# A delta-rule and gated-MLP kernel: filler stages beside lone tile stages, a higher fill level, and a smaller weight for the widening products in the planner

## The chip, the cores and the metric

The kernel runs on one core of one Trainium2 chip. The metric is the device time of one execution in microseconds. TensorE (PE) does the matmuls, VectorE (DVE), ScalarE (ACT) and GpSimd (POOL) the rest, and SyncE (SP) issues the DMAs.

## The reference

Four batches of eight heads, 768 positions, head size 48, and behind them a gated MLP with mixing over the positions:

```
k_n = k / (norm(k) + 1e-6)
for t in range(768):                         # per batch and head, state is 48x48
    y[t]  = q[t] @ state
    state = state + beta[t] * outer(k_n[t], v[t] - k_n[t] @ state)
x = y, heads side by side                    # (4, 768, 384)
h = relu(x @ w_in);  u, v = halves of h      # 1024 -> 512 and 512
v_n = (v - mean(v)) / sqrt(var(v) + 1e-6)
v_s = w_spatial @ v_n + b_spatial            # mixes the 768 positions
out = (u * v_s) @ w_out
```

## The kernel before

**Chunks and steps.** The positions are cut into 12 chunks of 64 for each batch, so there are 48 steps (a step is one chunk of one batch, with its eight heads), and a table sets their order. Four steps are a group. For each group the keys are normed (`norm`), `kk` multiplies the keys with themselves, and the triangular 64x64 matrices of the chunk are inverted: DVE solves 32x32 blocks row by row (`lanes`, lines 647 and 654, with its data taken through DRAM by DMA: `ad`, `la`, `w`, `wd`, `ta`), for the first group in 16x16 blocks (`lanes16`, lines 1158 and 1165), which `widen` puts together with small 32x16 and 16x16 products on TensorE (lines 1192 and 1203). A step then runs the stages e and f (they finish the inverse), a (keys by the state), b (the inverse by the values, tiles `kv,ta`), c (the new state), qk and d (the output). In each batch a stage a waits for the c of the chunk before it.

**Tile stages.** Each of these stages is a list of 8 matmuls (16 for d) of 64x64 tiles in float32, which all write one of four PSUM banks (`pt`, taken and given back through `Slots` by the name `st_s`), and DVE or ACT reads the bank. Each float32 matmul shows as two matmul records in the trace. The two heads of a pair lie on one diagonal of the 128x128 array or on the other, so a stage is of the kind "diag" or "anti". When one stage of each kind is ready, the planner issues the two lists interleaved, one matmul of this, one of that.

**The MLP** works in full 128x128 products: v (line 923), u (line 989), g (lines 1021 and 1024) and o (line 1076), as soon as their positions are through the steps, into the banks `pm` and later `pw`.

**The order** of all instructions comes from a planner in the kernel (`Line`), which holds a model of each engine's time and always issues what can begin first, so each engine's queue is fixed when the kernel is built. Its model of TensorE's clock is a sum over the last 3.4 us (`area`): a full product counts 2300 for each modelled microsecond, a tile matmul 1.3 times its columns, a filler 256. Above `HOT` (3050) it takes matmuls to last 1x, else 2x. Where it sees TensorE wait by more than 0.12 us, and `area` is under `FILL`, it puts in fillers (`keep_warm`, `idle`): 128x256 matmuls of ones into a free bank, which nobody reads.

Of the kernel before, what the change touches and what calls it, by code (L numbers as in the profile page):

```python
# [14 lines left out]
NB, NH, SEQ, HD = 4, 8, 768, 48  # L15
# [25 lines left out]
PAIR = 1.0  # L41
LOW = 3600
HOT = 3050
FILL = 4000


def step_order():
# [19 lines left out]
class Op:  # L67
# [4 lines left out]
    def __init__(self, eng, occ, lat, dep, due, kind=None, make=None):  # L72
        self.eng, self.occ, self.lat, self.dep, self.due = eng, occ, lat, dep, due
        self.kind, self.make = kind, make


class Line:
# [4 lines left out]
    def __init__(self, t0):  # L82
        self.t = dict.fromkeys(("PE", "DVE", "ACT", "POOL", "SP"), t0)
        self.done = {}
        self.jobs = []
        self.mode = "full"
        self.cur = 0
        self.hist = []
        self.idle = self.room = None

    def at(self, *names):
        done = self.done

        def when():
            t = 0.0
            for n in names:
                if n is None:
                    continue
                if n not in done:
                    return None  # L100
                t = max(t, done[n])
            return t

        return when
# [39 lines left out]
    def keep_warm(self, t):  # L144

        n = 0
        while t - self.t["PE"] > 0.12 and self.area(self.t["PE"]) < FILL:
            slow = self.slow(self.t["PE"])
# [8 lines left out]
    def tensor(self, e0, near):  # L157
        tiles = [f for f in near if f[1].kind != "full"]
        full = [f for f in near if f[1].kind == "full"]

        def first(fs):
            return min(fs, key=lambda f: (f[1].due(), f[0]), default=None)

        kinds = {k: [f for f in tiles if f[1].kind == k] for k in ("anti", "diag")}
        low = self.area(e0) < LOW
        room = self.room(2)
        old = [f for f in tiles if e0 - f[3] > HOLD and f[1].due() <= self.cur + URGENT]
        pick = first(full) if low else None
        if pick is None and all(kinds.values()) and room is not None and room <= e0 + 0.3:
            if self.mode == "tile" or not full or old or first(tiles)[1].due() <= self.cur + PAIR:  # L170
                pick = first(tiles)
        pick = pick or first(old) or first(full) or first(tiles)
        t, op, j, _ = pick
        self.keep_warm(t)
        t = max(t, self.t["PE"])
        change = 0.12 if (op.kind == "full") != (self.mode == "full") else 0.0
        slow = self.slow(t)
        if op.kind == "full":
            self.mode = "full"
            self.t["PE"] = t + change + op.occ * slow  # L180
            self.hist.append((self.t["PE"], op.occ * 2300))
            return self.grant(j, t + change + op.occ * slow + op.lat - op.occ)
        self.mode = "tile"
        other = kinds["anti" if op.kind == "diag" else "diag"]
        f = None
        if room is not None and room <= t + 0.2:
            f = first([f for f in other if f[0] <= t + 0.2])
        picked = [(op, j)]
        if f:
            picked.append(f[1:3])  # L190
            t = max(t, f[0], room)
        lists = [o.make() for o, _ in picked]
        act_ = sum(o.lat * len(x) for (o, _), x in zip(picked, lists))
        for k in range(max(map(len, lists))):
            for x in lists:
                if k < len(x):
                    x[k]()
        end = t + change + 0.056 * slow * max(map(len, lists))
        self.t["PE"] = end
        self.hist.append((end, act_))  # L200
        for _, k in picked:
            self.grant(k, end + 0.22)
# [6 lines left out]
def dve(dep, due, e, fast=1.0):  # L209
    return Op("DVE", 0.078 + 0.00104 * e * fast, 0.2 + 0.00104 * e * fast, dep, due)  # L210


def act(dep, due, e, each=0):
    o = 0.05 + 0.15 * each + 0.00098 * e
    return Op("ACT", o, 0.12 + o, dep, due)
# [23 lines left out]
def delta_rule_gated_mlp(  # L239
# [16 lines left out]
    def sb(name, *shape, dt=F32):  # L256
        return const.tile([128, *shape], dt, name=name)

    line = Line(T0)
# [3 lines left out]
    mpos = sb("mpos", CH)  # L263
# [87 lines left out]
    pws = [ps.tile([128, 512], F32, name=f"pw{i}") for i in range(2)]  # L351

    class Slots:
        def __init__(self, tiles):
            self.free = [(0.0, k, x) for k, x in enumerate(tiles)]

        def ready(self, n=1):
            return sorted(self.free)[n - 1][0] if len(self.free) >= n else None

        def take(self):  # L360
            f = min(self.free)
            self.free.remove(f)
            return f[1:]

        def give(self, x, t):
            self.free.append((t, *x))

    st_s = Slots([x[:, 0:256] for x in banks])
    line.room = st_s.ready
    ob_s = Slots([sb(f"ob{i}", DM) for i in range(1)])  # L370
    tmp_s, pm_s, xs_s, vh_s, ub_s = Slots(tmps), Slots(pms), Slots(xsb), Slots(list(zip(vhs, vls))), Slots(ubs)

    def both(*whens):
        def when():
            t = 0.0
            for w in whens:
                x = w()
                if x is None:
                    return None
                t = max(t, x)  # L380
            return t

        return when

    def on(t):
        return lambda: t

    def due(x):
        return lambda: x
# [7 lines left out]
    def rows_t(h):  # L397
        return slice(h * 64, h * 64 + 64)

    def rows_s(h):  # L400
        return rows_t(1 - h)

    UH = [(u, h) for u in range(NU) for h in range(2)]
# [7 lines left out]
    def psl(t, w):  # L411
        return t[:, : NU * w].rearrange("p (u e) -> p u e", e=w)

    def mm(*a, **k):
        return lambda: nc.tensor.matmul(*a, **dict(dict(start=True, stop=True), **k))  # L415

    def tiles_op(kind, dep, d, build, w):

        held = []

        def make():
            x = st_s.take()
            held.append(x)
            return build(psl(x[1], w))

        return Op("PE", 0, 1.3 * w, both(dep, st_s.ready), d, kind, make), held


    def load_w(buf, hi, lo, src, d):
# [74 lines left out]
    def ta_of(g):  # L504
        return tas[g % TG]
# [398 lines left out]
    xuse, vt, ut_t, g_t, todo, own = {}, {}, {}, {}, [], []  # L904
# [275 lines left out]
    def widen(s, buf, pi):  # L1180
        d = due(-5 + s)
        ta = ta_of(0)
        tr = buf[:, s % 2 * 256 : s % 2 * 256 + 256].rearrange("p (u t) -> p u t", t=CH)
        t = yield dve(at(("back", min(s, 1)), ("wp", s - 2) if s > 1 else None), d, 256)
        nc.vector.transpose(out=tr.rearrange("p u t -> p (u t)"), in_=ta[:, s].rearrange("p u t -> p (u t)"))
        t = yield Op("PE", 0.7, 1.0, both(on(t), pm_s.ready), d, "full")
        p = pm_s.take()
        pp, px = (p[1][:, o : o + 64].rearrange("p (u t) -> p u t", t=16) for o in (0, 64))
        for u in range(NU):
            for q in range(4):  # L1190
                r, c = q * 32, q % 2 * 32
                nc.tensor.matmul(
                    pp[r : r + 32, u], ta[r : r + 16, s, u, c : c + 32], tr[r : r + 16, u, c : c + 16],
                    start=True, stop=True,
                )
        done["wp", s] = t
        t = yield act(on(t), d, 64, 1)
        nc.scalar.mul(out=pi[:, s], in_=pp, mul=hm)
        t = yield Op("PE", 0.45, 0.75, on(t), d, "full")
        for u in range(NU):  # L1200
            for q in range(4):
                r, c = q * 32, q % 2 * 32
                nc.tensor.matmul(
                    px[r : r + 16, u], pi[r : r + 32, s, u], ta[r : r + 32, s, u, c + 16 : c + 32],
                    start=True, stop=True,
                )
        for q in range(4):
            r, c = q * 32, q % 2 * 32
            t = yield act(on(t), d, 64)
            nc.scalar.copy(out=ta[r : r + 16, s, :, c + 16 : c + 32], in_=px[r : r + 16])  # L1210
        pm_s.give(p, t)
        done["T", 0, s] = t
# [41 lines left out]


    def idle(t):
        free = [f[2][:, 0:256] for k in (pm_s, st_s) for f in k.free if f[0] <= t]
        if free:
            nc.tensor.matmul(
                free[0].rearrange("p (n t) -> p n t", t=128),  # L1260
                ones,
                ones.unsqueeze(1).broadcast_to([128, 2, 128]),
                start=True,
                stop=True,
            )
        return bool(free)

    line.idle = idle
    ET = mybir.EngineType
    with tc.manual_schedule(engines={ET.PE, ET.DVE, ET.Activation, ET.Pool, ET.SP}):  # L1270
        seen = {"s": 0, "g": 0}
# [75 lines left out]
```

## Time and profile before

| what | value |
|---|---|
| median of 3 runs | 564.54 us (561.43 to 565.8) |
| profiled execution | 563.41 us |
| its span, first to last instruction | 561.7 us |
| mean granted TensorE clock in the span | 0.917 |
| matmul records / weight loads | 9040 / 9040 |
| TensorE, VectorE, ScalarE, GpSimd busy | 500.4, 355.0, 218.9, 142.7 us |

The span is what the trace covers; 1.7 us of the execution lie around it. Matmuls are pipelined, and a busy TensorE may run at half or at full granted clock, which the row PEclk shows apart from the busy share.

### The profile page before, as it was taken

To read this page: it belongs to the slowest core of one execution; us is meant where nothing else is said; L and a number is where in the kernel's file an instruction comes from. 1 tells how busy PE (TensorE), PEld (TensorE's weight loads), DVE (VectorE), ACT (ScalarE), POOL (GpSimd) and SP (SyncE) were. 2 spreads that over 40 slices of the span, in tenths; PEclk is the share of its full clock that TensorE was granted. 3 is DMA by queue.
4 is the path that set the end of the run, shared out by engine and by line. 5 is a ranking of instruction groups with operands and counts; after the bars stand their busy time and mean duration, and the time that the engine had idled before them with its cause. 6 is when DMAs were issued, how large, how long until landed. Compare 5 with 4: busy or idle time off the path is not lost.

```text
span 561.7 us, 21394 instructions
## 1 busy us (share of the span) xinstructions
PE 500.4 (89%) x9040; PEld 451.8 (80%) x9040; DVE 355.0 (63%) x1434; ACT 218.9 (39%) x536; POOL 142.7 (25%) x212
## 2 busy tenths in 40 slices
PE   4936886987989989888989999999999999999997
PEld 4835775876777978788978789879987999898996
DVE  5899786976799978778958993258235341134210
ACT  3233433542636335423235645321256341137111
POOL 5534333653454341323213233311001000000000
PEclk8576695985989989989999999999999999999999
DMA  8687286768575738676865544461304010000001
GB/s 236 175 154 169 92 216 126 215 191 167 139 196 133 191 98 182 147 211 139 207 109 115 136 109 117 134 160 48 67 30 127 17 36 29 32 20 15 2 34 52
DMA packets 134252, 66.97 MB, mean 119 GB/s; under 512 B 105894, under 2 KB 123532, under 8 KB 134156
## 3 DMA queue, kind: packets, MB, share of 16 engines
q1 hardware_dynamic: 134156, 65.60, 47.9%
q8 instruction: 71, 1.16, 0.9%
q14 instruction: 25, 0.20, 0.1%
HBM read 50.11 MB, written 15.17 MB: 116 GB/s over the span
## 4 chain that ended last, share of the span: by engine, by line
PE 60%; DVE 16%; DMA 10%; ACT 4%; issue 4%; SPq 4%; POOL 1%; DVEq 0%; ACTq 0%
PE pt L415 20%; PE pm L1021 11%; PE pm L923 6%; PE pm L989 6%; PE pw L1021 5%; PE pm L1076 4%; PE pw L1076 3%; DVE pw L654 2%; DVE prod L647 2%; DMA knn<-in_k_nat 2%; PE pw L923 1%; DMA k<-in_kv_t 1%; DMA la<-ad 1%; SPq L631 1%; PE pw L989 1%
## 5 line engine op out<-in xcount | busy, mean ns | idle before, releaser
L654 DVE TENSOR_TENSOR pw<-pw,prod 128x96 f32<-128x96 f32 (+7 forms) x330 | 80.7, 250 | 4.6
L647 DVE TENSOR_TENSOR prod<-pw,la 128x126 f32<-128x126 f32 (+7 forms) x330 | 78.3, 242 | 7.9 <-ACT pw L641 2.9
L696 POOL TENSOR_TENSOR kv<-kv,cn 128x192 f32<-128x192 f32 x48 | 24.6, 513 | 142.8 <-DMA kv<-in_kv_t 122.8
L1021 PE MATMUL pm<-wsp_h,vh 128*128 128x256 f32 x204 | 60.2, 295 | 0.4 <-ACT vh L965 0.4
L415 PE MATMUL pt<-kv,st 48*64 48x64 f32 x768 | 55.5, 238 | 4.1 <-ACT ta L737 2.0
L1021 PE MATMUL pm<-wsp_h,vl 128*128 128x256 f32 x204 | 57.7, 283 | 0.2 <-DVE vl L969 0.2
L1021 PE MATMUL pm<-wsp_l,vh 128*128 128x256 f32 x204 | 57.7, 283 | 0.0
L415 PE MATMUL pt<-aq,us 64*64 64x64 f32 x768 | 53.4, 232 | 0.3 <-issue 0.3
L415 PEld LDWEIGHTS pt<-kv,st 48*64 48x64 f32 x768 | 44.0, 147 | 6.9 <-ACT ta L737 2.1
L415 PE MATMUL pt<-kv,ta 64*64 64x48 f32 x768 | 35.5, 231 | 10.4 <-DVE t L550 3.5
L415 PEld LDWEIGHTS pt<-aq,us 64*64 64x64 f32 x768 | 44.3, 148 | 0.4 <-issue 0.4
L415 PEld LDWEIGHTS pt<-kv,ta 64*64 64x64 f32 x768 | 29.7, 143 | 16.3 <-issue 5.8
L1038 DVE TENSOR_TENSOR tmp<-pm,ub 128x512 f32<-128x512 f32 x17 | 11.8, 691 | 48.8 <-PE pm L1024 48.8
L1057 ACT CAST gh<-tmp 128x512 fp32r<-128x512 f32 x24 | 14.8, 618 | 71.0 <-DVE tmp L1038 71.0
L415 PE MATMUL pt<-kv 48*64 48x64 f32 x768 | 35.7, 235 | 6.3 <-DVE t L546 4.7
L415 PE MATMUL pt<-k 48*64 48x64 f32 x640 | 29.4, 232 | 13.1 <-DVE nr L556 8.8
L1021 PEld LDWEIGHTS pm<-wsp_h,vh 128*128 128x128 f32 x204 | 38.8, 190 | 1.9 <-ACT vh L965 0.6
L415 PE MATMUL pt<-tn,ta 64*64 64x32 f32 x768 | 35.3, 234 | 5.2 <-DVE tn L711 3.8
L572 POOL TENSOR_TENSOR mc<-mpos,cn 128x256 f32<-128x256 f32 x46 | 28.6, 628 | 42.9 <-DVE ta L607 24.3
L1021 PEld LDWEIGHTS pm<-wsp_h,vl 128*128 128x128 f32 x204 | 39.0, 191 | 0.4 <-DVE vl L969 0.4
L1021 PEld LDWEIGHTS pm<-wsp_l,vh 128*128 128x128 f32 x204 | 39.0, 191 | 0.0
L415 PEld LDWEIGHTS pt<-tn,ta 64*64 64x64 f32 x768 | 30.7, 149 | 8.9 <-ACT wstage L442 3.8
(176 smaller groups left out, 1426.8 us busy)
## 6 DMA issues: line engine op xcount, KB each, us to landing
kv<-in_kv_t SPq DMA_DIRECT2D x48, 456.0 KB, 4.5
ad<-ta SPq DMA_DIRECT2D x24, 256.0 KB, 4.2
la<-ad SPq DMA_DIRECT2D x44, 128.0 KB, 4.4
out<-ob SPq DMA_DIRECT2D x24, 192.0 KB, 1.9
k<-in_kv_t SPq DMA_DIRECT2D x20, 224.0 KB, 3.9
knn<-in_k_nat SPq DMA_DIRECT2D x10, 384.0 KB, 5.6
wd<-w SPq DMA_DIRECT2D x22, 128.0 KB, 3.9
ta<-wd SPq DMA_DIRECT2D x44, 64.0 KB, 3.5
```

The costliest lines, as they stand in the source:

```text
L415: return lambda: nc.tensor.matmul(*a, **dict(dict(start=True, stop=True), **k))
L572: (nc.vector if t in (0, 2) else nc.gpsimd).tensor_tensor(out=mc, in0=mall, in1=cns[t // G][:, t % G, 1].unsqueeze(2).broadcast_to([128, N ...
L631: nc.sync.dma_start(out=las[g % 2][l0 : l0 + 32], in_=src[:, r0 : r0 + 32, r0 : r0 + 32])
L647: nc.vector.tensor_tensor(out=pr, in0=w[:, :n, j : j + 1].broadcast_to([128, n, m]), in1=la[:, j, j + 1 : 32].unsqueeze(1).broadcast_to([1 ...
L654: nc.vector.tensor_add(out=w[:, :n, j + 1 : 32], in0=w[:, :n, j + 1 : 32], in1=pr)
L696: nc.gpsimd.tensor_tensor(out=v, in0=v, in1=cns[s // G][:, s % G, 0].unsqueeze(2).broadcast_to([128, NU, HD]), op=ALU.mult)
L923: nc.tensor.matmul(p[1], a[:, kt, ts], w[:, kt, DH:], start=(n == 0), stop=(n == 3 * NK - 1))
L989: nc.tensor.matmul(pu[:, k], w[:, kt, d0 : d0 + 128], a[:, kt], start=(n == 0), stop=(n == 3 * NK - 1))
L1021: nc.tensor.matmul(pg[:, k], v[:, d0 : d0 + 128], w[:, si, ts], start=(n == 0), stop=False)
L1038: nc.vector.tensor_tensor(out=gt, in0=pg, in1=ut[:, hs], op=ALU.mult)
L1057: nc.scalar.copy(out=gh[:, hs], in_=gt)
L1076: nc.tensor.matmul(p[1][:, :DM], a[:, dd, ts], w[:, dd], start=(n == 0), stop=(n == 3 * ND - 1))
```

## The change

Four edits, all in the planner and in what it issues:

- `FILL` goes from 4000 to 5000.
- A tile stage that is issued without a partner, while `area` is under the new `FAKE` (5500), gets a filler stage (`fake`): as many matmuls of the mask `mpos` by itself, on the other diagonal, interleaved, into a free bank that nobody reads. That bank keeps a tag, and until it is taken again only stages of the same kind may take it; the general fillers leave it out.
- A stage therefore asks for a bank that fits its kind (`ready_for`), and a pair for two that fit (`ready_both`).
- The two products of `widen` count 150 instead of 2300 for each modelled microsecond in `area`.

```
-FILL = 4000
+FILL = 5000
+FAKE = 5500
...
-        room = self.room(2)
+        room = self.room()
...
-            self.hist.append((self.t["PE"], op.occ * 2300))
+            self.hist.append((self.t["PE"], op.occ * (op.make or 2300)))
...
+        if not f and self.area(t) < FAKE:
+            more = self.fake("anti" if op.kind == "diag" else "diag", t, len(lists[0]))
+            if more:
+                lists.append(more)
+                act_ += 62 * len(more)
...
+        def fit(self, kind):
+            return sorted(f for f in self.free if self.tag.get(f[1], kind) == kind)
...
+        def ready_both(self):
+            a, d = self.fit("anti"), self.fit("diag")
+            t = [max(x[0], y[0]) for x in a for y in d if x[1] != y[1]]
+            return min(t) if t else None
...
-        def take(self):
-            f = min(self.free)
+        def take(self, kind=None):
+            f = min(self.free) if kind is None else self.fit(kind)[0]
             self.free.remove(f)
+            self.tag.pop(f[1], None)
             return f[1:]
...
-        t = yield Op("PE", 0.7, 1.0, both(on(t), pm_s.ready), d, "full")
+        t = yield Op("PE", 0.7, 1.0, both(on(t), pm_s.ready), d, "full", 150)
...
-        t = yield Op("PE", 0.45, 0.75, on(t), d, "full")
+        t = yield Op("PE", 0.45, 0.75, on(t), d, "full", 150)
...
+    def fake(kind, t, n):
+        fit = [f for f in st_s.fit(kind) if f[0] <= t]
+        own = [f for f in fit if f[1] in st_s.tag]
+        if not own and (kind in st_s.tag.values() or len(st_s.free) < 2):
+            return None
+        f = (own or fit or [None])[-1]
+        if f is None:
+            return None
+        st_s.tag[f[1]] = kind
+        p = psl(f[2], HD)
+        r = [
+            mm(p[rows_t(h) if kind == "diag" else rows_s(h), u], mpos[rows_t(h)], mpos[rows_t(h), 0:HD])
+            for u, h in UH
+        ]
+        return (r * 2)[:n]
```

In the whole program the fillers of ones go from 152 to 253, and 29 filler stages (232 matmuls of `mpos`) come in; every other matmul is there as often as before. Since the planner's model changes, all queues after the first microseconds are in another order. Three places on TensorE's queue follow; lines of the changed kernel are 23 higher there (438 is 415 of before, 1215 and 1226 are 1192 and 1203, 1282 is 1259).

Near the start, behind the two products qk of the first steps (`kv_167`, `kv_168`), where the keys of the second group (`xs`) are multiplied. Before:

```order
L415 MATMUL pt_203<-kv_167 64x64 x8
L415 MATMUL pt_204<-kv_168 64x64 x8
L1259 MATMUL pm_207<-ones 128x256 x11
L415 MATMUL pt_205<-xs 64x64 x8
L415 MATMUL pt_203<-xs 64x64 x8
L1259 MATMUL pm_207<-ones 128x256 x6
L415 MATMUL pt_206<-xs 64x64 x8
L1259 MATMUL pm_207<-ones 128x256
L415 MATMUL pt_204<-xs 64x64 x8
```

And now:

```order
L438 MATMUL pt_204<-kv_168 64x64 x8
L1282 MATMUL pm_207<-ones 128x256 x17
L438 MATMUL pt_205<-xs 64x64
L438 MATMUL pt_204<-mpos 64x48
L438 MATMUL pt_205<-xs 64x64
```

The fillers ahead of the next kk went from 11 to 17, and that kk has a filler stage beside it, whose rows alternate with its own.

Ahead of and within `widen` of the first group (lines 1192 and 1203 before), which ends the preparation of the first step. Before:

```order
L1259 MATMUL pm_207<-ones 128x256 x16
L415 MATMUL pt_205<-k 64x64 x8
L1192 MATMUL pm_207<-ub_150,ta_177 32x16 x16
L1192 MATMUL pm_208<-ub_150,ta_177 32x16 x16
L1203 MATMUL pm_207<-ta_177,ub_150 16x16 x16
L1203 MATMUL pm_208<-ta_177,ub_150 16x16 x16
L415 MATMUL pt_203<-k 64x64 x8
L1192 MATMUL pm_207<-ub_150,ta_177 32x16 x16
L1192 MATMUL pm_208<-ub_150,ta_177 32x16 x16
L415 MATMUL pt_206<-tn_175,ta_177 64x32 x8
L1203 MATMUL pm_207<-ta_177,ub_150 16x16 x16
L415 MATMUL pt_204<-tn_176,ta_177 64x32 x8
```

And now:

```order
L1282 MATMUL pm_207<-ones 128x256 x20
L1215 MATMUL pm_207<-ub_150,ta_177 32x16 x16
L1282 MATMUL pm_208<-ones 128x256 x6
L1226 MATMUL pm_207<-ta_177,ub_150 16x16 x16
L1215 MATMUL pm_208<-ub_150,ta_177 32x16 x16
L1282 MATMUL pt_206<-ones 128x256 x2
L1215 MATMUL pm_207<-ub_150,ta_177 32x16 x16
L1226 MATMUL pm_208<-ta_177,ub_150 16x16 x16
L1226 MATMUL pm_207<-ta_177,ub_150 16x16 x16
L438 MATMUL pt_204<-tn_175,ta_177 64x32
L438 MATMUL pt_206<-k 64x64
L438 MATMUL pt_204<-tn_175,ta_177 64x32
```

A run of 20 fillers now stands directly ahead of it, where a kk did (with 16 fillers ahead of that kk), 8 fillers stand within it, and its products come one step at a time instead of two steps together.

Behind stage b (`kv_168,ta_180`) of the step that is 13th counted from 0, the second of the second batch. Before:

```order
L1259 MATMUL pm_207<-ones 128x256 x5
L415 MATMUL pt_204<-kv_168,ta_180 64x48 x8
L415 MATMUL pt_206<-k 64x64 x8
L415 MATMUL pt_205<-tn_176,ta_180 64x32 x8
L415 MATMUL pt_204<-us_116,kv_168 64x48 x8
L1259 MATMUL pm_207<-ones 128x256
L415 MATMUL pt_205<-kv_168,st_112 64x64 x2
```

And now:

```order
L438 MATMUL pt_206<-kv_168 64x64 x8
L438 MATMUL pt_204<-kv_168,ta_180 64x48 x8
L1282 MATMUL pm_207<-ones 128x256 x10
L438 MATMUL pt_203<-kv_169 64x64 x8
L438 MATMUL pt_205<-us_116,kv_168 64x48 x8
L1282 MATMUL pm_207<-ones 128x256 x3
L438 MATMUL pt_204<-k 64x64 x8
L1282 MATMUL pm_207<-ones 128x256 x17
L946 MATMUL pm_207<-win_h,xh 128x512 x3
```

Thirty fillers stand between that b and the next product of the MLP (line 946, 923 before), where one stood behind b and five ahead of it.

More of the change, by code (lines that the diff above doesn't have):

```diff
@@ L88, in __init__ @@
         self.hist = []
-        self.idle = self.room = None
+        self.idle = self.room = self.fake = None
     def at(self, *names):
@@ L355, in __init__, with ready_for @@
             self.free = [(0.0, k, x) for k, x in enumerate(tiles)]
+            self.tag = {}
+        def fit(self, kind):
+            return sorted(f for f in self.free if self.tag.get(f[1], kind) == kind)
         def ready(self, n=1):
             return sorted(self.free)[n - 1][0] if len(self.free) >= n else None
-        def take(self):
-            f = min(self.free)
+        def ready_for(self, kind):
+            f = self.fit(kind)
+            return f[0][0] if f else None
+        def ready_both(self):
[4 more added lines that the diff above has]
+            f = min(self.free) if kind is None else self.fit(kind)[0]
             self.free.remove(f)
+            self.tag.pop(f[1], None)
             return f[1:]
@@ L368, in delta_rule_gated_mlp @@
     st_s = Slots([x[:, 0:256] for x in banks])
-    line.room = st_s.ready
+    line.room = st_s.ready_both
     ob_s = Slots([sb(f"ob{i}", DM) for i in range(1)])
@@ L421, in make @@
         def make():
-            x = st_s.take()
+            x = st_s.take(kind)
             held.append(x)
             return build(psl(x[1], w))
-        return Op("PE", 0, 1.3 * w, both(dep, st_s.ready), d, kind, make), held
+        return Op("PE", 0, 1.3 * w, both(dep, lambda: st_s.ready_for(kind)), d, kind, make), held
     def load_w(buf, hi, lo, src, d):
@@ L1256, in idle @@
     def idle(t):
-        free = [f[2][:, 0:256] for k in (pm_s, st_s) for f in k.free if f[0] <= t]
+        free = [f[2][:, 0:256] for k in (pm_s, st_s) for f in k.free if f[0] <= t and f[1] not in k.tag]
         if free:
@@ L1266, in idle @@
         return bool(free)
-    line.idle = idle
+    def fake(kind, t, n):
[13 more added lines that the diff above has]
+        return (r * 2)[:n]
+    line.idle, line.fake = idle, fake
     ET = mybir.EngineType
```

## Prediction

> **What bounds the kernel now.** I read the page first (size, busy shares, granted clock, chain), then the windows by stage, then the stretches at half clock, and at last what the chain holds in them.
>
> ```profile
> span 561.7 us, 21394 instructions
> PE 500.4 (89%) x9040; PEld 451.8 (80%) x9040; DVE 355.0 (63%) x1434; ACT 218.9 (39%) x536; POOL 142.7 (25%) x212
> PEclk8576695985989989989999999999999999999999
> PE 60%; DVE 16%; DMA 10%; ACT 4%; issue 4%; SPq 4%; POOL 1%; DVEq 0%; ACTq 0%
> ```
>
> TensorE is the engine to look at: 89% busy and 60% of the chain that ended last. But its clock digit is under 9 in most of the first 12 slices and almost always 9 later. So the kernel has two regimes, and the windows (span, then busy of PE, PEld, DVE, ACT, POOL, then granted clock) show where they meet:
>
> ```profile
> 0.00:61.50 61.50, 38.56 (x656) 35.28 (x658) 49.85 (x184) 19.59 (x54) 25.48 (x66) 0.67 0.74 176
> 61.50:151.60 90.10, 74.69 (x1700) 65.05 (x1699) 68.48 (x305) 41.20 (x106) 39.51 (x46) 0.79 0.70 168
> 151.60:354.80 203.20, 187.88 (x4021) 166.60 (x4021) 163.13 (x722) 89.69 (x222) 68.26 (x86) 0.97 0.62 146
> 354.80:482.40 127.60, 124.54 (x2113) 113.03 (x2112) 53.86 (x178) 45.10 (x106) 9.49 (x14) 1.00 0.26 71
> 482.40:561.70 79.30, 74.77 (x560) 71.82 (x560) 19.65 (x47) 23.32 (x50) 0.00 (x0) 0.99 0.08 27
> ```
>
> The stretches end at stage b of step 0, 12, 35 and 47. Up to 61.5 us VectorE is the fuller engine (49.85 of 61.50 us). From 354.8 us on TensorE is 96% busy at a clock of 0.99 to 1.00, and both orders hold the same work there: behind step 35 the same products within one or two stages, behind step 47 the same o, g, v and u, with 12 more fillers of ones and one filler stage. **So those last 207 us move as a block.** What the change can win or lose is when step 35 is reached, and most of that lies before 250 us, where the clock is at half (the third column from the end is the granted clock):
>
> ```profile
> 48.17:65.24 17.07, 12.26 (x423) 11.18 (x425) 13.21 (x55) 9.00 (x31) 3.84 (x6) 0.50 0.51 118
> 68.65:72.07 3.42, 3.29 (x94) 3.33 (x96) 2.17 (x13) 0.84 (x3) 2.28 (x4) 0.50 0.26 71
> 85.72:99.37 13.65, 10.02 (x150) 9.00 (x151) 9.47 (x48) 5.38 (x13) 5.57 (x7) 0.50 0.67 130
> 123.27:140.33 17.06, 13.07 (x275) 11.79 (x271) 10.36 (x35) 5.59 (x17) 4.70 (x8) 0.50 0.84 195
> 164.23:171.05 6.82, 5.94 (x71) 4.54 (x70) 6.58 (x23) 2.01 (x6) 4.52 (x5) 0.50 0.84 168
> 198.36:201.77 3.41, 3.41 (x91) 3.11 (x87) 2.25 (x12) 0.89 (x4) 2.18 (x3) 0.50 0.00 0
> 246.15:249.56 3.41, 3.41 (x121) 3.41 (x112) 2.31 (x8) 1.65 (x6) 0.51 (x1) 0.50 0.55 159
> ```
>
> Busy time at half clock is not all on the path. The chain's shares, asked for the stretch 10.63 to 27.69 us (also half clock) and for these seven in turn, say how much is:
>
> ```profile
> by line: PE pt L415 24.4%; PE pm L1259 15.5%; DVE ta L607 11.7%; DVE mc L572 7.1%; issue 6.8%; DVE ss L539 5.8%; DVE ub L454 4.8%; DVE wstage L458 4.8%; POOL wstage L462 4.3%; DVE ub L460 2.2%; DVE wstage L460 2.0%; DVE wstage L454 2.0%; DV
> by line: PE pt L415 46.0%; issue 21.8%; PE pm L1192 14.8%; PE pm L1203 7.5%; ACT ub L1198 3.8%; PE pm L1259 3.0%; DVE ub L1185 2.6%; DVE prod L647 1.7%; DVE pw L654 0.2%
> by line: PE pt L415 98.4%; DVE prod L647 3.5%; issue 0.8%
> by line: DMA la<-ad 26.8%; SPq L631 26.0%; PE pm L923 14.7%; PE pt L415 14.5%; SPq L869 11.1%; SPq L872 6.9%; issue 3.8%; ACT win_h L464 2.9%; SPq L692 2.8%; ACT ta L737 1.3%; ACTq L641 0.3%
> by line: DMA xd<-xs 35.3%; DMA xs<-xd 18.7%; PE pt L415 18.4%; PE pm L923 14.1%; DVE t L546 10.4%; issue 6.3%; DVE us L772 2.2%; SPq L872 1.9%; DVE kv L756 1.7%; ACT nr L541 1.3%; DVE t L550 0.6%; DVE t L548 0.4%; ACT xh L888 0.2%; ACTq L44
> by line: PE pt L415 43.5%; PE pm L923 41.9%; issue 9.6%; ACT wstage L442 6.2%; ACT pi L725 3.9%
> by line: PE pt L415 72.3%; PE pm L1021 27.7%
> by line: PE pt L415 102.4%
> ```
>
> Without the fillers (L1259) TensorE holds 24.4% of 17.06 = 4.2 us, then 68.3% of 17.07 = 11.7, 3.4, 29.2% of 13.65 = 4.0, 32.5% of 17.06 = 5.5, 85.4% of 6.82 = 5.8, 3.4 and 3.4: 41.4 us of the path at half clock. At full clock that would be half, so 20.7 us is the most that the clock alone can give on this path.
>
> **The change part by part.** First the prices: timeline rows of 16 fillers at full and at half clock, then windows (PE busy, records, clock) around a pair at full clock, a pair at half, a lone stage at full and a lone stage at half.
>
> ```profile
> 81.44 2.17 PE L1259 MATMUL pm<-ones 128*128 128x256 f32 x16
> 41.94 3.41 PE L1259 MATMUL pm<-ones 128*128 128x256 f32 x16
> 66.15:66.90 0.75, 0.71 (x33) 1.00 0.56 102
> 134.40:135.60 1.20, 1.10 (x32) 0.50 1.41 184
> 144.20:144.92 0.72, 0.72 (x18) 1.00 0.18 57
> 21.80:22.95 1.15, 1.15 (x18) 0.50 0.44 45
> ```
>
> *Filler stages.* A pair takes 0.71 us where a lone stage takes 0.72, and 1.10 where it takes 1.15 (a neighbour's record or two is in each window). So 29 filler stages cost about nothing on TensorE. The reserved bank could make a real stage wait or go alone; counting the orders, tile slots (the longer list of each pair) from step 12 on are 1560 before and 1576 now, 16 more at 0.71/16 us each, 0.7 us; before step 12 they are 712 and 696, 0.7 us less. Sum 0.
>
> *Fillers of ones.* One costs 2.17/16 = 0.14 us at full and 3.41/16 = 0.21 us at half clock where nothing else had to be waited for, and 0 in a real wait. 101 more are 14 to 21 us if no wait covers them; 54 of them stand before step 0. Near the start the run ahead of the fifth kk grows from 11 to 17, and the 15.5% of L1259 in the first chain row (2.6 us) shows that run on the path. I charge 6 x 0.21 = 1.3 us, less half of what the 3 fewer fillers ahead of the seventh kk give back (0.6): **+1.0 us** (bounds 0 and 1.3).
>
> *Widening and steps 0 to 2.* This is 48.17 to 72.07 us, 11.7 + 3.4 us of path at half clock. What waits for it, and how step 4 begins:
>
> ```profile
> DVE us L772 <- ACT ta L1210: 2.9, 1, 2.9
> 87.23 1.05 PE L415 MATMUL pt<-tn,ta 64*64 64x32 f32 x15 [3.62 <-DVE tn L711]
> 54.74 0.94 PE L1192 MATMUL pm<-ub,ta 16*32 16x16 f32 x55 [1.72 <-issue]
> q8 instruction: 71, 1.16, 0.9%
> ```
>
> Step 4 needs the second group's inverse, which VectorE works out in `lanes`; VectorE stands still for 2.9 us for step 0's b, so a faster widening also reaches step 4, but only up to about that wait, since the rest of `lanes` and its DMAs don't get shorter. The new order has fillers within the widening, but only 8, and two pairs of e and f with kk; steps 1 and 2 get 24 filler matmuls and 13 of ones. I take half of 11.7/2 and all of 3.4/2: 2.9 + 1.7 = **-4.6 us** (bounds 0, if step 4 waits anyway, and -7.5).
>
> *Steps 3 to 5, 85.72 to 99.37 us.* The path there is DMA and SP's queue (26.8 + 26.0 + 11.1 + 6.9%). The order has 9 fillers of ones in step 3, ahead of that wait, where 20 stood: the clock should fall again. **0** (bound -2.0).
>
> *Steps 8 and 9, 123.27 to 140.33 us.* 54% of the path is the DMA through `xd`, which stays. Three filler stages now stand ahead of step 8, 9 fillers in it and 2 filler stages in step 9; half of 5.5/2: **-1.3 us** (bounds 0 and -2.7).
>
> *Step 13, 164.23 to 171.05 us.* Thirty fillers take 4.2 us at full and 6.4 us at half clock. The wait at this place:
>
> ```profile
> 162.00 0.67 PE L415 MATMUL pt<-kv,ta 64*64 64x48 f32 x16 [1.15 <-DVE kv L756]
> 165.29 0.48 PE L415 MATMUL pt<-kv,st 48*64 48x64 f32 x4 [0.88 <-ACT pi L725]
> ```
>
> With the 0.88 us of idling ahead of its d I see 2 us of wait now, so 30 fillers overrun it by 2 us unless the wait has grown; they do lift the clock, 5.8/2 = 2.9. **-0.9 us** (bounds -2.9 and +3.5). At 198 and 246 us nothing is put in: 0 (bound -3.4 together).
>
> Sum: +1.0 - 4.6 - 1.3 - 0.9 = -5.8 us. The profiled execution of 563.41 us (span 561.7) becomes 557.6; the median of the runs, 564.54, is 1.1 us higher, so I forecast **558.5 us** for a median. A measurement of this kernel can tell about 1%, 5.6 us, from no change.
>
> **Does denser mean faster here?** The windows below are three stretches of tile stages and one of fillers, each one clock period long and each fully busy at half clock:
>
> ```profile
> 123.27:126.68 3.41, 3.41 (x77) 0.50 0.98 332
> 126.68:130.09 3.41, 3.41 (x95) 0.50 0.69 204
> 61.83:65.24 3.41, 3.41 (x88) 0.50 0.03 8
> 24.28:27.69 3.41, 3.41 (x21) 0.50 0.44 93
> ```
>
> After the first two the clock stayed at half, after the other two it rose. The Trainium skill, page "TensorE: Matmul & The Clock Gate", section "What's actually happening", says that one busy window of about 3.4 us brings the full clock. By that rule the first two would have lifted it, and a filler stage would bring nothing beside a stage that keeps TensorE busy anyway; the trace differs, so the measurement decides. But the rows don't carry the filler stages far either: 95 records in a period are nearly three full pairs, and even they did not lift the clock, while the fourth window, nearly all fillers, was followed by a full one. So filler stages should hold a clock that is up better than they raise one, which is why I halve terms above.
>
> **Rivals.** *(1) No change that can be measured.* TensorE is faster, but steps wait for `lanes`, `xd` and SP's queue as before. For it: the 3.62 us wait ahead of step 4, the DMA shares above. Against it: VectorE's own 2.9 us wait for TensorE. Without the -4.6 the sum is -1.2: 563.3 us. A variant: only the fillers of ones count, since a lone stage keeps TensorE as long as a pair (0.72 against 0.71 us); then the 1.7 and the 1.3 fall away, and it is 564.5 - 2.8 = 561.7 us, chance 0.08 of the 0.20 below. The Trainium skill's rule above would lead to this. *(2) The clock stays up nearly everywhere.* All 20.7 us less the 1.0: 545 us. For it: fillers did raise the clock at 24.28 us. Against it: the 3.62 us wait ahead of step 4 stays, with fewer fillers ahead of it than now, and 54% of the path around step 9 is DMA. *(3) Slower: fillers in front of work that is ready.* A run of fixed length can't be left when its wait ends early. Place: the 54 before step 0 and the 30 of step 13. Price 0.14 to 0.21 us each. It decides when more than 11.4 us of the 14 to 21 are uncovered, which eats the gain of 5.8 and 5.6 more; with all of them uncovered and half the gain, 564.5 + 17 - 3 = 578 us; at the point itself 570. Against it: before step 0 TensorE is busy for only 38.56 of 61.50 us. *(4) The change doesn't raise the clock*, since stages beside fillers stay below what lifts it: then 1.0 us and the overrun of 2 are left, 567.5 us. *(5) Instruction loading:* 565 more matmul records (101 and twice 232) with their loads are 1130 instructions; 71 loads served 18080, so 4.4 more. One load without cover cost 1.72 us (the row above); all without cover 7.6 us. I count it as part of the width upwards.
>
> **How the numbers follow.** The forecast, between 553 and 561 us: 0.40. Rival 2, down to 543: 0.12. Rival 1 and the like, 561 to 565: 0.20. Rival 4 with some of 5, up to 570: 0.16. Rival 3 beyond 570: 0.12. Faster by over 1% (below 558.9) is rival 2 and 0.35 of the forecast's 0.40, together 0.47; slower by over 1% (above 570.2) is rival 3 with 0.09 for loading on top of 4, 0.21; the rest, 0.32, is within 1%. The range for 8 in 10 is 543 to 573, from rival 2's end to a third of the way into rival 3. The likeliest case's own is 553 to 561.
>
> **What would show it.** Right: granted clock between 48 and 72 us above 0.8 (now 0.50 for most of it), step 4's first e before 84 us instead of 87.23, step 35's b about 6 us before 354.8, and the last 79.3 us unchanged. Wrong: fillers of L1282 on the chain before step 0 or in step 13; 126 to 140 us still at half clock; or a step 35 that comes no earlier though the clock is up, which would mean that VectorE or DMA had the path. The forecast fails altogether if the new order of VectorE's or SP's queue delays the first `lanes`.

## The result and the profile after

The changed kernel takes 561.13 us (median of 20 runs, 555.3 to 566.47) where the kernel before takes 564.98 us (20 runs beside them, 560.24 to 568.45). The ratio is 0.9917, 95% interval 0.989 to 0.9944: 0.8% or 3.9 us faster. Ratios here and below leave out executions over 1.5% slower than the fastest of their kernel, medians in us do not, so that late_fill12 below has a ratio from 4 of its 12 runs beside a median of 563.01 us, and no profile is read of it and of widen_only, whose profiled execution was such a one. The profiled execution takes 559.02 us with a span of 557.3 us, 4.4 us below the span before. First the page of the changed kernel: size, busy shares, granted clock, chain and instruction loads.

```profile
span 557.3 us, 22530 instructions
PE 509.1 (91%) x9605; PEld 460.0 (83%) x9605; DVE 355.2 (64%) x1436; ACT 216.9 (39%) x536; POOL 140.7 (25%) x210
PEclk9777586897999999899999999999999999999999
PE 65%; DVE 16%; DMA 7%; issue 4%; ACT 3%; SPq 3%; POOL 0%; DVEq 0%; ACTq 0%
q8 instruction: 75, 1.23, 0.9%
```

TensorE is busier because of 565 more records, the clock digits are better in places only, and four more instruction loads (queue q8) were needed. Where the time came from shows in the same stretches as before (cut at stage b of steps 0, 12, 35 and 47; span, busy of PE, PEld, DVE, ACT, POOL, then granted clock):

```profile
0.00:61.50 61.50, 41.61 (x923) 37.91 (x923) 51.02 (x187) 19.77 (x54) 27.29 (x68) 0.78 0.76 177
61.50:151.40 89.90, 79.02 (x1876) 69.31 (x1876) 71.86 (x319) 41.30 (x107) 39.18 (x45) 0.81 0.67 168
151.40:353.70 202.30, 189.31 (x4164) 167.65 (x4163) 159.75 (x715) 88.89 (x223) 67.37 (x86) 0.99 0.65 152
353.70:477.70 124.00, 123.49 (x2065) 111.86 (x2064) 52.89 (x172) 43.41 (x102) 6.85 (x12) 1.00 0.22 65
477.70:557.30 79.60, 75.72 (x588) 73.29 (x588) 19.66 (x47) 23.56 (x51) 0.00 (x0) 0.99 0.08 27
```

Against the rows of before the stretches changed by 0, -0.2, -0.9, **-3.6** and +0.3 us: together -4.4. Nearly all of it lies behind step 35, where the clock was full in both kernels. There TensorE's waits differ (total, times, longest; three rows of before, 354.8 to 482.4 us, then the only one of after, 353.7 to 477.7 us):

```profile
PE pt L415 <- issue: 1.7, 2, 1.4
PE pt L415 <- DVE kv L756: 0.9, 1, 0.9
PE pt L415 <- ACT pi L725: 0.5, 1, 0.5
```

```profile
PE pt L438 <- DVE kv L779: 0.5, 1, 0.5
```

Before, TensorE stood for 127.60 - 124.54 = 3.1 us there, which these three rows sum to; now it stands for 124.00 - 123.49 = 0.5 us. That is 2.6 of the 3.6 us. The 1.4 us among the three is a wait for an instruction load: the trace has one on queue q8 from 367.30 to 368.50 us, and the wait ends 1.37 us behind it. The other 1.0 us is busy time: 48 records fewer, although a filler stage is among them, since the new order has done about four more tile stages before step 35. So that 1.0 us was earned earlier and only shows here.

Early on, the clock is what the prediction looked at. Windows of its half-clock stretches between 45 and 150 us:

```profile
47.81:75.12 27.31, 20.86 (x630) 18.77 (x632) 23.53 (x105) 12.29 (x42) 9.22 (x14) 0.50 0.57 122
88.77:102.42 13.65, 12.06 (x234) 10.06 (x234) 8.97 (x40) 6.20 (x15) 6.96 (x8) 0.50 0.51 136
126.31:133.14 6.83, 6.30 (x160) 6.02 (x162) 3.60 (x22) 3.38 (x9) 1.87 (x2) 0.50 0.34 68
```

The first is longer than before (17.07 and 3.42 us in two pieces), the second the same 13.65 us, the third 10 us shorter.

### The profile page after: what moved, and what is told of

The parts are those of the page before. It is cut to its first block, busy times and chain, and to the rows that moved or that the text cites. A ratio compares the mean times of both kernels' runs of the same rounds, so it can differ in the third digit from the quotient of the medians.

```text
span 557.3 us, 22530 instructions
## 1 busy us (share of the span) xinstructions
PE 509.1 (91%) x9605; PEld 460.0 (83%) x9605; DVE 355.2 (64%) x1436; ACT 216.9 (39%) x536; POOL 140.7 (25%) x210
## 4 chain that ended last, share of the span: by engine, by line
PE 65%; DVE 16%; DMA 7%; issue 4%; ACT 3%; SPq 3%; POOL 0%; DVEq 0%; ACTq 0%
PE pt L438 22%; PE pm L1044 12%; PE pw L1044 6%; PE pm L1012 6%; PE pm L946 5%; PE pm L1099 5%; PE pw L1099 3%; DVE prod L670 3%; DVE pw L677 3%; DMA kv<-in_kv_t 2%; DMA la<-ad 2%; PE pm L1282 2%; PE pw L946 2%; PE pw L1012 1%; DMA ad<-ta 1%
## 5 line engine op out<-in xcount | busy, mean ns | idle before, releaser
L670 DVE TENSOR_TENSOR prod<-pw,la 128x96 f32<-128x96 f32 (+10 forms) x330 | 78.3, 241 | 13.4 <-ACT pw L664 8.8
L677 DVE TENSOR_TENSOR pw<-pw,prod 128x96 f32<-128x96 f32 (+9 forms) x330 | 81.1, 249 | 4.6
L1044 PE MATMUL pm<-wsp_h,vh 128*128 128x256 f32 x192 | 57.0, 297 | 0.0
L1044 PE MATMUL pm<-wsp_l,vh 128*128 128x256 f32 x192 | 54.2, 282 | 0.6 <-issue 0.6
L1044 PE MATMUL pm<-wsp_h,vl 128*128 128x256 f32 x192 | 54.0, 281 | 0.0
L1282 PE MATMUL pm<-ones 128*128 128x256 f32 x215 | 40.6, 339 | 3.2 <-ACT ones L282 2.5
L438 PE MATMUL pt<-ta,pi 64*64 64x32 f32 x768 | 36.2, 235 | 5.1 <-issue 3.9
L595 POOL TENSOR_TENSOR mc<-mpos,cn 128x256 f32<-128x256 f32 x46 | 28.3, 628 | 43.1 <-DVE cn L583 24.8
L438 PEld LDWEIGHTS pt<-st,kv 48*64 48x64 f32 x704 | 26.9, 141 | 13.8 <-issue 3.7
L1282 PEld LDWEIGHTS pm<-ones 128*128 128x128 f32 x215 | 33.8, 231 | 5.3 <-ACT ones L282 2.5
L868 ACT ACTIVATE xs<-pt 112x256 f32<-112x256 f32 x48 | 18.3, 381 | 50.7 <-PE pt L438 40.1
```

Of the source, the lines that this page charges most:

```text
L595: (nc.vector if t in (0, 2) else nc.gpsimd).tensor_tensor(out=mc, in0=mall, in1=cns[t // G][:, t % G, 1].unsqueeze(2).broadcast_to([128, N ...
L670: nc.vector.tensor_tensor(out=pr, in0=w[:, :n, j : j + 1].broadcast_to([128, n, m]), in1=la[:, j, j + 1 : 32].unsqueeze(1).broadcast_to([1 ...
L677: nc.vector.tensor_add(out=w[:, :n, j + 1 : 32], in0=w[:, :n, j + 1 : 32], in1=pr)
L868: nc.scalar.mul(out=xt[0:112, :, qt * 64 : qt * 64 + 64], in_=psl(held[0][1], CH)[0:112], mul=-1.0)
L1044: nc.tensor.matmul(pg[:, k], v[:, d0 : d0 + 128], w[:, si, ts], start=(n == 0), stop=False)
L1282: nc.tensor.matmul(free[0].rearrange("p (n t) -> p n t", t=128), ones, ones.unsqueeze(1).broadcast_to([128, 2, 128]), start=True, stop=True,)
```

## The experiments

Two theories. **A**: the gain comes from the clock, which the fillers hold up. **B**: it comes from the other order of the queues (the planner's thresholds, its tags on banks and its counts throw all engines' orders into another one), and the fillers themselves bring nothing.

A kernel can keep the planner's whole order and still issue no filler: the planner counts the filler, and the matmul is left out. That is called mute below. Fillers go to banks that nobody reads. Each was timed in 5 rounds beside the kernel before on the same chip; the ratio is always to that.

A table of the profiles first (one execution each), since the readings below rest on it. The span is split in three: **work** is the time in which TensorE has a record that isn't a filler, taken at full clock; **clock** is what the half clock adds to that (half of such time in stretches at 0.50); **gaps** are the rest, idle or filler only. Half clock is taken to double a product's time; the 16 fillers of the prediction took 3.41 us at half and 2.17 us at full clock, so the clock column is at the high end and work at the low end.

| kernel | ratio, 95% interval | span | b of steps 0, 12, 35, 47 at | work | clock | gaps |
|---|---|---|---|---|---|---|
| before | 1 | 561.7 | 61.5, 151.6, 354.8, 482.4 | 443.4 | 29.7 | 88.6 |
| before_mute | 0.994 (0.9899 to 0.9981) | 561.6 | 57.5, 148.6, 355.6, 482.6 | 439.4 | 44.3 | 77.9 |
| before_late8 | 0.9995 (0.9957 to 1.0034) | 563.6 | 57.6, 148.5, 355.1, 484.3 | 440.6 | 39.5 | 83.5 |
| fill_only | 1.006 (1.0022 to 1.0098) | 569.7 | 57.8, 157.0, 350.5, 489.9 | 440.8 | 35.2 | 93.8 |
| no_fake | 1.012 (1.0059 to 1.0181) | 574.1 | 60.9, 156.6, 355.1, 494.2 | 442.4 | 37.1 | 94.6 |
| fake_only | 1.0126 (1.0075 to 1.0177) | 566.9 | 61.9, 154.3, 348.6, 487.9 | 446.3 | 25.2 | 95.5 |
| widen_only | 0.9942 (0.9904 to 0.9981) | | | | | |
| after | 0.9917 (0.989 to 0.9944) | 557.3 | 61.5, 151.4, 353.7, 477.7 | 446.4 | 20.9 | 89.9 |
| fake_mute | 0.9935 (0.9889 to 0.998) | 557.3 | 60.4, 151.0, 353.2, 477.7 | 444.1 | 24.8 | 88.3 |
| all_mute | 0.9897 (0.9846 to 0.9947) | 556.9 | 57.9, 147.1, 353.7, 478.0 | 440.6 | 40.1 | 76.1 |
| early_fill | 0.9982 (0.9943 to 1.0021) | 560.3 | 60.7, 148.9, 356.6, 481.4 | 441.8 | 37.2 | 81.2 |
| late_fill | 0.9871 (0.9811 to 0.9931) | 556.5 | 59.8, 147.9, 352.7, 476.8 | 443.4 | 28.4 | 84.7 |
| late_fill8 | 0.9855 (0.9799 to 0.9912) | 552.4 | 58.7, 147.1, 347.8, 472.8 | 441.1 | 32.2 | 79.2 |
| late_fill12 | 0.9857 (0.9801 to 0.9912) | | | | | |

The trace has no clock record before the first change of the clock, and the page counts such time as full. In the kernels that leave out early fillers that is a long time, and products show that it was half: the same 16 records of `k` take 1.12 us in all_mute at the start and 0.68 us in the changed kernel at a granted clock of 1.00. (One row of each kernel's timeline.)

```profile
22.38 1.12 PE L438 MATMUL pt<-k 48*64 48x64 f32 x16 [1.25 <-DVE ta L630]
```

```profile
164.56 0.68 PE L438 MATMUL pt<-k 48*64 48x64 f32 x16
```

So the printed mean clocks of these kernels are too high. The table counts the time ahead of the first record as half clock: 98.6 us in all_mute, 69.3 to 81.5 us in the late kernels, 18.1 us in before_mute, 5.7 to 8.5 us in the others.

### Parts of the change alone

fill_only: the kernel before with

```
-FILL = 4000
+FILL = 5000
```

> The kernel before with FILL at 5000 alone: no filler stages, the widening counted as before. Theory A (the gain comes from clock that the added fillers keep up behind step 12): a part of the gain, 562 to 564 us against 565 before, and the half-clock stretches between 151 and 250 us (10.2 and 3.4 us before) shrink. Theory B (the gain comes from the other order of the queues, not from the fillers): any time between 559 and 568, without a link to the half-clock time.

Measured: 570.89 us, ratio 1.006, above the range of either theory. The higher level alone, with the order that it brings, makes the kernel slower.

no_fake: the changed kernel without filler stages.

```
-FAKE = 5500
+FAKE = 0
```

> The changed kernel with FAKE at 0: FILL 5000 and the widening counted small, no filler stages and no reserved bank. Theory A: fillers of ones carry the gain, so 561 to 562 us, like the changed kernel. If filler stages are what counts: 564 to 565. Theory B: 559 to 568, whatever the half-clock time.

Measured: 574.0 us, ratio 1.012, again above both ranges, with the clock at half from 49.1 to 103.7 us.

fake_only and widen_only: the filler stages with their kept banks alone (`FILL` 4000, the widening counted as before), and the small count of the widening alone (150 in the kernel before).

> Of the change only the filler stages with their kept banks: the threshold of the ones stays at 4000 and the widening counts as before. Theory A (fillers carry the gain): between the two kernels, 561 to 564 us, since the stages fill tile gaps of steps 3 to 35. Theory B (the order counts, and each edit throws the queues into another order): anything from 557 to 575 us, and the total follows the half clock and the gaps of TensorE before step 35, not the number of fillers.

> Of the change only the widening's small products counted as small (150 for 2300), threshold of the ones 4000, no filler stages. Theory A: more fillers around 48 to 61 us, the rest as before: 562 to 566 us. Theory B: another order from step 0 on, 557 to 575 us, again as the half clock and the gaps before step 35 come out.

Measured: 571.68 us, ratio 1.0126, and 563.97 us, ratio 0.9942. One by one the three parts give +0.6, +1.3 and -0.6%, the first and third together +1.2%, and all three -0.8%. The parts don't add up, and the clock alone doesn't explain it: fake_only has 4.5 us less of half-clock loss than the kernel before and is slower, with gaps 6.9 us larger. The slower ones lose behind step 35: from its b to step 47's they take 139 us where the changed kernel takes 124. The window from step 35's b to step 47's shows it best in fill_only:

```profile
350.50:489.90 139.40, 136.77 (x2171) 125.06 (x2170) 58.09 (x192) 53.02 (x123) 12.51 (x16) 1.00 0.25 67
```

It reached step 35 3.2 us earlier than the changed kernel but has 136.77 us of TensorE work up to step 47 where that has 123.49, at full clock: the planner had left more of the work for later, some 90 records of the MLP's products above all. An early step 35 is worth nothing by itself; what counts is how much of TensorE's fixed work has been put into the waits by then.

### The changed order without fillers

fake_mute, where a filler stage is planned and not issued:

```
-        return (r * 2)[:n]
+        return [lambda: None] * n
```

> The changed kernel's order of all queues, but the matmuls of the 29 filler stages are planned and not issued. If the filler stages do the work of the change, the half-clock time before 140 us grows by a clock period or more and the time by 2 us or more (563 and up). If they do nothing, 561 us within 0.4%, and the waits of TensorE for its instructions fall, since 464 matmul records with as many weight loads are gone.

Measured: 563.08 us, ratio 0.9935, the same as the changed kernel within the intervals; every stretch of the table ends within 1.1 us of it. TensorE's waits without a releaser fell from 12.6 to 6.4 us, as expected, and steps 13 to 22 came 2.8 to 6.0 us earlier, but from step 23 on no more than 0.6 us of that is left. **The 29 filler stages bring nothing that can be measured.**

all_mute, where the fillers of ones are left out as well:

```
-        if free:
-            nc.tensor.matmul(
...
         return bool(free)
```

> The changed kernel's order of all queues with no filler issued at all, neither the filler stages nor the matmuls of ones. Theory A: TensorE is at half clock for most of the first 150 us and in the gaps behind, half-clock time rises from 82 us to 130 or more, and the time is 6 to 15 us longer, 567 to 576. Theory B: the order is what counts, and the time stays at 561 to 563.

Measured: 560.05 us, ratio 0.9897. With no filler at all, this order is still 0.5 to 1.5% faster than the kernel before. **Theory A falls.** Half-clock time did grow as it said, from 68 us in the changed kernel's clock records (the expectation says 82) to some 132 us, but the time didn't. The table says how: without fillers the half clock costs 40.1 - 20.9 = 19.2 us more, but gaps shrink by 13.8 and work by 5.8 us. The fillers give back what they take. They take it early. The two kernels' shares of the chain up to 61.5 us in before and after (they read: line and share of the stretch) show the fillers in it, L1259 with 4.3% and L1282 with 9.0%:

```profile
by line: PE pt L415 14.2%; issue 11.8%; DMA ub<-in_k_nat 10.4%; DVE ta L607 5.7%; DVE ub L1165 5.6%; DVE ub L1158 4.9%; PE pm L1259 4.3%; PE pm L1192 4.1%; DVE ss L539 3.3%; DVE prod L647 2.8%; DVE pw L654 2.4%; PE pm L1203 2.1%; DVE mc L57
```

```profile
by line: DMA kv<-in_kv_t 15.8%; PE pm L1282 9.0%; DMA la<-ad 6.7%; issue 6.3%; DVE prod L670 5.8%; DVE pw L677 5.5%; SPq L613 4.1%; DVE ta L630 3.9%; DVE wstage L477 3.4%; PE pt L438 3.2%; DVE wstage L481 3.0%; DVE ss L562 2.5%; DVE wstage 
```

That is 2.6 us and 5.5 us of fillers on the path. Without any, step 0 begins at 57.9 us and step 12 at 147.1, although TensorE runs at half clock up to 98.6 us.

### The order before without fillers, and with late ones

before_mute (the kernel before, fillers planned and not issued) and before_late8 (its fillers issued only behind step 8's b):

```
-        if free:
+        if free and ("b", 8) in done:
```

> The kernel before in its own order, with no filler issued at all (the planner still counts them, so that every engine's order stays). Theory B (the order of the changed kernel brings its gain, fillers of either kind pay as much early as they return late): step 0's b moves from 61.5 us to about 58, steps 12 to 20 lose about as much to the half clock, and the total is within 3 us of the kernel before, ratio 0.995 to 1.005, so that the two kernels without fillers stand about 4 to 5 us apart, as those with fillers do. Theory A (the fillers carry the gain): taking them all away costs more here, 570 us or above.

> The kernel before in its own order, its fillers of ones issued only behind the b of step 8. If the early fillers cost about as much in either order: step 0's b at 57.5 to 58.5 us (61.5 with all fillers), half clock behind step 12 no longer than the 12.6 us of all fillers, total 558 to 560 us, ratio about 0.990, some 3 us behind the changed kernel with the same choice (556.3 us, 0.9855). If the gain of the late start is one of the changed order alone: 563 us or more. If the order is worth nothing: 556 us.

Measured: 562.92 us, ratio 0.994, and 565.13 us, ratio 0.9995. In this order too the fillers gain nothing: leaving them out costs 14.6 us of clock and gives back 10.7 us of gaps and 4.0 of work. The same waits stand behind step 35 without fillers (before_mute, 355.6 to 482.6 us), so they come with the order and not with a filler:

```profile
PE pt L415 <- issue: 1.9, 2, 1.4
PE pt L415 <- DVE kv L756: 0.9, 1, 0.9
PE pt L415 <- ACT pi L725: 0.5, 1, 0.5
```

The table bears this out over all its profiles: from step 35's b to step 47's the six kernels in the changed order take 124.0 to 125.0 us, the three in the order before 127.0 to 129.2, whatever fillers they have.

Of before_late8's three expectations the second came true: the early start came (step 0 at 57.6 us), and was lost again by step 35. I had expected 558 to 560 us.

### When fillers pay

In the changed kernel, fillers of both kinds only behind step 0's b (late_fill), only behind step 8's (late_fill8), only behind step 12's (late_fill12), or only up to step 0's (early_fill):

```
-        if free:
+        if free and ("b", 8) in done:
...
-        return (r * 2)[:n]
+        return (r * 2)[:n] if ("b", 8) in done else [lambda: None] * n
```

> The changed kernel in its own order; no filler is issued before the b of step 0 is planned, all of them after it. If the fillers' early cost and their late return are two separate things: step 0's b at about 58 us as without any filler (61.5 with all), the clock behind step 12 as with all fillers, 557 to 559 us, ratio about 0.985. If the early start is lost again by a wait further on (a state stage that waits for data or for the MLP's work): step 12's b at 151 us as with all fillers, and 561 us, ratio 0.993.

> As the run before, but fillers start only behind the b of step 8 (124 to 127 us). If the clock between steps 0 and 8 doesn't matter for the end: step 12's b at about 147 us as with no filler, steps 12 to 20 without their half-clock stretch, 556 to 558 us. If fillers between steps 0 and 8 hold work that is needed later: no better than 560 us.

> The changed kernel in its own order, with fillers only up to the b of step 0 and none behind it. If the early cost and the late return are separate: step 0's b at 61.5 us as with all fillers, half clock in steps 12 to 20 as with none, 563 to 564 us, ratio 0.995 to 1.0. If neither matters: 560 to 561 us.

> The changed kernel in its own order, fillers of both kinds only behind the b of step 12 (147 to 151 us). If the fillers matter only where the state chain has caught up with the data, behind step 12: step 12's b at 147 us, no half clock between 150 and 215 us, 555 to 557.5 us, ratio about 0.986, as with fillers from step 8 on. If those between steps 8 and 12 carried a part: 558 to 560 us, step 12's b at 149 us or later. If the 0.9855 of the other start was an accident of that chip: 560 us, ratio 0.99.

Measured: 558.03, **556.34**, 563.77 and 563.01 us; ratios 0.9871, 0.9855, 0.9982 and 0.9857. Early fillers alone keep little or nothing of the gain, late ones alone keep it: the intervals of early_fill and late_fill8 lie apart. That late fillers are better than none is not shown: all_mute's 0.9897 overlaps with the three late ratios, and in the order before the late ones (0.9995) did no better than none (0.994). Windows of the stretches from step 12's b to 35's and from there to 47's, for before_late8 and then late_fill8:

```profile
148.50:355.10 206.60, 189.85 (x4021) 168.59 (x4021) 162.57 (x722) 89.79 (x222) 68.26 (x86) 0.96 0.61 144
355.10:484.30 129.20, 124.62 (x2113) 112.96 (x2112) 54.15 (x178) 45.07 (x106) 9.60 (x14) 1.00 0.27 71
```

```profile
147.10:347.80 200.70, 190.06 (x4164) 168.78 (x4163) 159.10 (x714) 88.85 (x223) 66.98 (x86) 0.98 0.66 154
347.80:472.80 125.00, 123.62 (x2064) 111.91 (x2063) 53.01 (x172) 43.40 (x102) 6.86 (x12) 1.00 0.22 64
```

With fillers from the same step on, the changed order is 5.9 us shorter between steps 12 and 35 and 4.2 us behind that, and the two ratios' intervals lie apart. These two kernels also differ in how many fillers they have (12.1 us of the span are covered by fillers alone, against 4.2 us), so the pair shows what order and late fillers do together, not the order alone. late_fill8 is the best version that ran: clearly ahead of the kernel before, and by 0.6% ahead of the changed one, which their intervals don't quite separate.

**What stays open.** The pure comparison of the orders, all_mute against before_mute, is 4.6 us in the profiles' spans (556.9 against 561.6) but 0.9897 against 0.994 in the ratios, whose intervals overlap. So the stretch behind step 35 is shorter by the order, but how much of the 0.8% of the whole kernel the order gives is not settled: the ratios alone allow nothing as well as all of it, and the rest would be that the old order's fillers hurt it (0.994 without them). What in the new order took the waits behind step 35 away can't be laid to one of the three parts: two of them alone are slower, and of widen_only no profile here shows that stretch. widen_only's 0.9942 overlaps with the whole change's 0.9917, so what the other two parts add to it is open too.

## Why the prediction was right, and where it wasn't

The size was close (-5.8 us forecast, -3.9 measured) and the direction right, by a sum of which the largest term was wrong. That was luck: up to step 35, where all the terms lie, the change won 1.1 us (2.1 with the stages done earlier), and the rest came from where I had put nothing. The measured 561.13 us lies just beyond the likeliest case's own 553 to 561, in what I had given to rival 1.

- **"Those last 207 us move as a block": failed, and this is where the gain was.** They shrank from 206.9 to 203.6 us. I had counted the products behind step 35 as the same within one or two stages, where the new order has about four fewer, and had not asked what TensorE waits for there. The 3.1 us of waits were in the trace before.
- **Widening and steps 0 to 2, -4.6 us: failed.** Granted clock between 48 and 72 us stayed at 0.50, step 0 began at 61.5 us as before, and step 4's first e at 86.71 us where I had asked for 84:

```profile
86.71 1.22 PE L438 MATMUL pt<-tn,ta 64*64 64x32 f32 x32 [1.51 <-DVE tn L734]
```

  The 20 fillers ahead of the widening ran from 42.67 us on, but behind them TensorE stood still for 5.7 us up to 51.06 us for VectorE (the first row of waits below), and within that wait, at 47.81 us, the clock fell: the fillers ended too early to bridge it. My price was too high as well: by the prediction's own rows (0.72 against 1.15 us, 0.71 against 1.10, 2.17 against 3.41) full clock saves 35 to 37% of the time at half clock, where I took half. Whether a better clock would have helped steps 0 to 4 no run shows, as none held it up between 48 and 72 us; the bound of 0 that I gave ("if step 4 waits anyway") is near what came. And all_mute, at half clock up to 98.6 us, is earlier than the changed kernel at the b of every step from 0 to 32. Three clock periods of the changed kernel (PE alone) show that the 8 fillers among small products, which all lie in the first of them, weren't enough:

```profile
51.22:54.64 3.42, 3.42 (x104) 0.50 0.98 119
...
68.29:71.71 3.42, 3.42 (x79) 0.50 0.20 47
71.71:75.12 3.41, 3.41 (x88) 0.50 0.93 178
```

  All three are fully busy; after the first two the clock stayed at half, after the third it rose. The rule of the Trainium skill ("TensorE: Matmul & The Clock Gate", "What's actually happening"), that one busy window brings the full clock, again isn't borne out here by these rows.
- **Fillers of the lead-in, +1.0 us: the mechanism right, its level missed.** They stand on the chain with 5.5 us where I had 2.6 of before. I priced only the six more of them, and step 0 began no later than before. All fillers together put off step 0 by 3.6 us in this order and 4.0 in the old one (61.5 against 57.9 and 57.5), so part of rival 3, fillers in front of work, was there in both kernels.
- **Steps 8 and 9, -1.3 us: the clock came, the time didn't.** The half-clock stretch shrank from 17.06 to 6.83 us, but a wait for an instruction load stood in front of it. Waits of TensorE up to 130 us:

```profile
PE pm L1215 <- DVE ub L1208: 5.7, 1, 5.7
...
PE pt L438 <- issue: 5.1, 3, 3.5
```

  The wait of 3.5 us ends at 126.84 us, without a releaser; step 8's b came at 127.1 us (124.1 before), step 12's at 151.4 (151.6). The trace shows the load: one on queue q8 from 124.41 to 125.40 us, and the wait ends 1.44 us behind it, as the six waits of over 1.2 us without a releaser in the trace before end 1.2 to 1.5 us behind one. The count of loads rose from 71 to 75, as rival 5 had worked out (4.4 more). The load isn't the whole of it: in fake_mute no such wait stands ahead of step 8's b, which comes at 123.0 us, but step 10's b comes at 144.3 us, where it was 144.2 before and 144.8 in the changed kernel. What holds step 10 in all three stays open.
- **Step 13, -0.9 us: the clock was full, as forecast**, and step 20's b came 2.7 us earlier; by step 35 only 1.1 us of it was left. Steps 3 to 5, which I had put at 0, had 13.65 us at half clock as before.
- **The likeliest rival** (1, no change since steps wait for something else) describes the first 354 us well: there the change won 1.1 us.

## What to carry to other kernels

Where TensorE is the bound and its work is fixed, split the span into work, loss by half clock and gaps, and price a change in all three: fillers that saved 19 us of half clock here cost 20 us in gaps and drawn-out work. In a lead-in that another engine sets, fillers put off the first step by 3.6 to 4.0 us here, so leave them out there; whether they pay anywhere later is not shown. A planner's constant that is turned by a little reorders every queue and moved the time here by anything from -0.8 to +1.3%, so compare orders with their own fillers taken out before crediting a mechanism, and look for waits also in the stretches that seem full.

## What the runs showed of the hardware that was not expected

- A kernel at half clock for its first 98.6 us was no slower at the end: all_mute (560.05 us) is no slower than the changed kernel (561.13 us), which is at full clock for most of 20 to 48 us. TensorE was busy for only 20.83 of the first 57.90 us, VectorE for 49.70; the third column from the end prints full clock, but this stretch lies before the first clock record:

```profile
0.00:57.90 57.90, 20.83 (x576) 18.70 (x577) 49.70 (x184) 19.88 (x54) 27.31 (x68) 1.00 0.80 187
```

- TensorE can stand still for an instruction load, and once for 3.5 us, twice the 1.72 us that the trace before showed; the clock fell to half near the end of that wait, from 126.31 to 133.14 us. In the traces of before and after each of the eleven waits of 1.0 us or more without a releaser ends 1.2 to 1.6 us behind a load of queue q8.
- A mean granted clock can mislead: all_mute prints 0.972 and the changed kernel 0.941, though the first has 80.2 us of its products at half clock and the second 41.8.
